# A spectral convolution and two gated MLPs on one core: output tiles through the two input buffers, sums of weight blocks in smaller pieces

## The chip, the cores and the metric

The kernel runs on one core of one Trainium2 chip. The metric is the device time of one execution in microseconds (us), the median of several runs. Engines are named as in the profile: PE is TensorE's matmul, PEld its weight load, DVE VectorE, ACT ScalarE, POOL GpSimd, SP SyncE, which here issues nearly all DMAs.

## The reference

```python
X = np.fft.rfft(x, axis=1)                    # x: 2 x 3008 x 256
y = np.fft.irfft(X * (filt_r + 1j * filt_i), n=3008, axis=1)
x = y.reshape(6016, 256)
gate = 1.0 / (1.0 + np.exp(-(x @ w_gate)))    # w_gate, w_val: 256 x 1536
x = gate * (x @ w_val) @ w_out                # first MLP
h = x @ w_in                                  # w_in: 256 x 2048
g = h * (1.0 / (1.0 + np.exp(-1.702 * h)))
out = g @ w_out2                              # second MLP
```

## The kernel before

Tokens lie along the free dimension in 12 tiles of 512 or 480 columns. The convolution of the first batch comes first, the first MLP over its tiles and beside it the convolution of the second batch follow, and from about 710 us on the second MLP runs alone. Each product of 128 rows is made of three matmuls (`mm3`, lines 120 to 122): every float32 operand is held as a high part, made by ACT (line 116), and a remainder, the low part, made by POOL or DVE (line 117).

The second MLP takes the tiles in six pairs `p`, and for each pair the 2048 rows of `w_in` in eight sets `fp` of two blocks. The two by two blocks of a set are multiplied with seven products in place of eight: `prod(o, k, first)` adds product `k` to one of the four banks `x`, `z`, `y`, `w`. Their left sides are blocks of `w_in` and sums of such blocks (`w_parts`, `combine_w`); their right sides are input tiles and sums of input tiles (`x_parts`, `combine_x`). A set then has four results, each a `Block`: `sig` is ACT's sigmoid of the bank into `sg`, `mul` is DVE's product of bank and `sg` (line 742), `parts` the split into high (ACT) and low (POOL), and `back(c)` the product of the result with a block of `w_out2`, added to the accumulator `accs[j][c]`. The eight `back` products of a set run between the seven `prod` of the next, so the last ones of a pair run in set 0 of the next pair.

PE, ACT, DVE and POOL keep the order of the program in this stage (it is under `manual_schedule`), and SP does so everywhere. Before this stage a planner orders the other engines.

When the last `back(0)` of a tile is done, ACT copies the accumulator into the output tile `outs[t]`, for `back(1)` DVE does, and SP sends each half out (lines 753 to 759). That tile has the tag `o` with `bufs=1`: one buffer, which the tile's two halves share, and which the next tile's copies get once its DMAs are done. The inputs of a pair are read by `load_x2` into tiles of the tag `yraw`, which has two buffers (`new_raw`, line 405): SP is asked for the next pair's in set 1, and `combine_x` reads them from set 3 on.

The sums that `combine_w` and `combine_x` make are spread over the sets as `chores`, a list of steps. `chore()` takes the next step; it stands at three places of a set: place 1 after the previous set's last `parts`, place 2 after `bz.parts`, place 3 after `bw.parts`. `combine_w` for the weights of sets 0 to 4 is called in the last tile of the first MLP, all steps at once; for sets 5 to 7 its steps are appended in sets 0, 1 and 2 of pair 0. The twelve steps of `combine_x` for the next pair are appended in set 3 of pairs 0 to 4. The tiles that `combine_w` and `combine_x` use for their intermediate sums have the same tags, `ex` and `c`, with one buffer each.

Of the kernel before, what the change touches and what calls it, by code (L numbers as in the profile page):

```python
# [8 lines left out]
F32 = mybir.dt.float32  # L9
# [3 lines left out]
AF = mybir.ActivationFunctionType  # L13
# [4 lines left out]
P = 128  # L18
# [69 lines left out]
def kernel(  # L88
# [12 lines left out]
    nc = tc.nc  # L101
# [3 lines left out]
    work = ctx.enter_context(tc.tile_pool(name="work", bufs=2))  # L105
# [13 lines left out]
    def mm3(o, w, x, first, last, **kw):  # L119
        nc.tensor.matmul(out=o, lhsT=w[0], rhs=x[0], start=first, stop=False, **kw)  # L120
        nc.tensor.matmul(out=o, lhsT=w[0], rhs=x[1], start=False, stop=False, **kw)  # L121
        nc.tensor.matmul(out=o, lhsT=w[1], rhs=x[0], start=False, stop=last, **kw)  # L122
# [248 lines left out]
    nt = len(tiles)  # L371
    pos = [0]
# [31 lines left out]
    def new_raw():  # L404
        return work.tile([P, 2, 512], F32, tag="yraw", name="yraw")
# [17 lines left out]
    def load_x2(t):  # L423
        raw = new_raw()
        nc.sync.dma_start(out=raw, in_=xscr[t].rearrange("(c p) n -> p c n", p=P))
        return raw
# [37 lines left out]
    def w_parts(fp):  # L464
        f0, f1 = slice(2 * fp * P, (2 * fp + 1) * P), slice((2 * fp + 1) * P, (2 * fp + 2) * P)

        def spare(k):
            a, b = divmod(3 * fp + k, 8)
            c, d = divmod(b, 4)
            return [e[:, c, d * P:(d + 1) * P] for e in extra[a]]  # L470

        a11, a12, a22, s1 = ([w[:, c, f] for w in wi] for c, f in ((0, f0), (1, f0), (1, f1), (0, f1)))
        return a11, a12, spare(2), a22, s1, spare(0), spare(1)

    def combine_w(fp):
        fs = slice(2 * fp * P, (2 * fp + 2) * P)
        v = stage[0].tile([P, 2, 2, P], F32, tag="ex", name="wv")
        r = stage[0].tile([P, 4, P], F32, tag="c", name="wr")
        q = w_parts(fp)
        dst = q[4], q[5], q[6], q[2]  # L480

        def sums():
            nc.vector.tensor_add(v.rearrange("p c i f -> p c (i f)"), *[w[:, :, fs].bitcast(F32) for w in wi])
            nc.vector.tensor_add(r[:, 0], v[:, 0, 1], v[:, 1, 1])
            nc.vector.tensor_sub(r[:, 1], r[:, 0], v[:, 0, 0])
            nc.vector.tensor_sub(r[:, 2], v[:, 0, 0], v[:, 0, 1])
            nc.vector.tensor_sub(r[:, 3], v[:, 1, 0], r[:, 1])

        def hi():
            for k in range(4):  # L490
                nc.scalar.activation(out=dst[k][0], in_=r[:, k], func=AF.Copy)

        def lo():
            for k in range(4):
                nc.vector.tensor_sub(dst[k][1], r[:, k], dst[k][0].bitcast(F32))  # L495

        return [sums, hi, lo]

    def x_parts(p):
        if p % 2 == 0:  # L500
            at = [[w[:, k].rearrange("p v c f -> p (v c f)") for w in wg] for k in range(7)]
        else:
            at = [[w[:, 7 + k].rearrange("p v c f -> p (v c f)") for w in wg] for k in range(5)]
            at += [[w[:, 2 * k:2 * k + 2, :].rearrange("p a b -> p (a b)") for w in wo] for k in range(2)]
        return at

    def combine_x(p, raw):
        n = tiles[2 * p][3]
        (b11, b21), (b12, b22) = ([r[:, c, :n] for c in range(2)] for r in raw)
        dst = [[w[:, :n] for w in d] for d in x_parts(p)]  # L510
        u, v = (stage[0].tile([P, 512], F32, tag=k, name="xs")[:, :n] for k in ("ex", "c"))

        def hi(k, src):
            nc.scalar.activation(out=dst[k][0], in_=src, func=AF.Copy)

        def lo(k, src):
            nc.vector.tensor_sub(dst[k][1], src, dst[k][0].bitcast(F32))

        sub = nc.vector.tensor_sub
        return [  # L520
            lambda: hi(0, b11),
            lambda: (lo(0, b11), hi(1, b21)),
            lambda: (lo(1, b21), hi(2, b22)),
            lambda: lo(2, b22),
            lambda: sub(u, b12, b11),
            lambda: (sub(v, b22, u), hi(4, u)),
            lambda: (lo(4, u), hi(5, v)),
            lambda: lo(5, v),
            lambda: sub(b12, b22, b12),
            lambda: (sub(u, b21, v), hi(6, b12)),  # L530
            lambda: (lo(6, b12), hi(3, u)),
            lambda: lo(3, u),
        ]
# [113 lines left out]
    for t in range(2, nt):  # L647
        for f in range(FC1):
            steps = []
            if pools is not None:  # L650
                k, odd = divmod(unit, 2)
# [54 lines left out]
            if f in (0, 2, 4, 6, 8):  # L706
                for step in combine_w(f // 2):
                    step()
            if f == 6:
                raw = [load_x2(u) for u in range(2)]  # L710
            if f == 8:
                sums = combine_x(0, raw)
# [16 lines left out]
    outs = {}  # L729

    class Block:
# [15 lines left out]
        def back(self, c):  # L747
            t, n, f = self.t, self.n, 2 * self.fp + self.i
            last = self.fp == FC2 // 2 - 1 and self.i == 1
            cs = slice(c * P, (c + 1) * P)  # L750
            acc = accs[self.j][c][:, :n]
            mm3(acc, [w[:, f, cs] for w in wp], self.gp, self.fp == 0 and self.i == 0, last)
            if last:
                if c == 0:
                    outs[t] = work.tile([P, 2, 512], F32, tag="o", name="o", bufs=1)
                    nc.scalar.copy(outs[t][:, 0, :n], acc)  # L756
                else:
                    nc.vector.tensor_copy(outs[t][:, 1, :n], acc)
                nc.sync.dma_start(out=out[c * P:(c + 1) * P, pos[t]:pos[t] + n], in_=outs[t][:, c, :n])

    backs = [pend[0], None, pend[1]]
    chores = []
# [8 lines left out]
    def chore():  # L771
        if chores:
            chores.pop(0)()

    for p in range(nt // 2):
        n = tiles[2 * p][3]
        for fp in range(FC2 // 2):
            z, y, w, x = (ps[(nset + k) % 4][:, :n] for k in (1, 2, 3, 0))
            g = gring[nset % 2 * 4:nset % 2 * 4 + 4]
            bz, by, bw, bx = (  # L780
                Block(i, j, p, fp, o, q) for (i, j), o, q in zip(((0, 0), (0, 1), (1, 1), (1, 0)), (z, y, w, x), g)
            )
            nset += 1
            lhs, rhs = w_parts(fp), x_parts(p)

            def prod(o, k, first):
                mm3(o, lhs[k], [r[:, :n] for r in rhs[k]], first, True, skip_group_check=True)

            if p == 0 and fp < 3:
                chores += combine_w(5 + fp)  # L790
            if p + 1 < nt // 2:
                if fp == 1:
                    raw = [load_x2(2 * p + 2 + u) for u in range(2)]
                if fp == 3:
                    chores += combine_x(p + 1, raw)

            prod(x, 0, True)
            if prev:
                prev.mul()
            nc.scalar.copy(s1[:, :n], x)  # L800
            back()
            if prev:
                prev.parts()
            chore()
            prod(z, 1, True)
            back()
            nc.vector.tensor_add(z, z, s1[:, :n])
            bz.sig()
            prod(y, 4, True)
            bz.mul()  # L810
            prod(x, 5, False)
            nc.scalar.copy(s5[:, :n], y)
            nc.scalar.copy(s2[:, :n], x)
            back()
            bz.parts()
            chore()
            prod(y, 2, False)
            nc.vector.tensor_add(y, y, s2[:, :n])  # L818
            by.sig()
            back()  # L820
            prod(x, 6, False)
            nc.vector.tensor_add(w, x, s5[:, :n])  # L822
            bw.sig()
            back()
            by.mul()
            by.parts()
            back()
            bw.mul()
            bw.parts()
            back()  # L830
            chore()
            prod(x, 3, False)
            bx.sig()
            back()
            prev = bx
            backs = [lambda o=o, c=c: o.back(c) for o in (bz, by, bw, bx) for c in range(2)]
    prev.mul()
# [43 lines left out]
```

## Time and profile before

| | |
|---|---|
| median of 3 runs | 1220.15 us (1218.12 to 1223.8) |
| the profiled execution | 1219.74 us |
| its span, first to last instruction | 1217.8 us |
| PE busy | 1169.5 us, 96% |
| DVE, ACT, POOL busy | 681.5 us (56%), 659.0 us (54%), 573.4 us (47%) |
| mean granted clock of TensorE | 0.99 |

The profile is of one execution. Busy times are unions over the engine's instructions; matmuls are pipelined, and their modelled ends reach into the next one's start. A wait is the idle time of an engine before an instruction, put down to what ended it.

### The profile page before, as it was taken

The page shows a single profiled execution, that of the slowest core. Times are in us where ns is not written, and L with a number is a line of the kernel's source. Part 1 is how long each engine was busy: PE and PEld are TensorE (multiplying, and loading weights), DVE is VectorE, ACT ScalarE, POOL GpSimd, SP SyncE. Part 2 cuts the span into 40 slices and gives each one's busy share as a digit, 9 for nine tenths or more (in the row PEclk, how much of TensorE's full clock was granted, in tenths as well). Part 3 has the DMA queues.
Part 4 walks back from the last instruction along what each step waited for, and adds up shares of the span by engine and source line. Part 5 has one row for each costly group of instructions (what it writes and reads, how often), then busy time and mean ns, then how long its engine had stood idle before and what let it go on. Part 6 is the DMA issues. An engine that isn't in the chain of part 4 may idle for free.

```text
span 1217.8 us, 14310 instructions
## 1 busy us (share of the span) xinstructions
PE 1169.5 (96%) x5072; PEld 951.0 (78%) x5072; DVE 681.5 (56%) x1055; ACT 659.0 (54%) x1171; POOL 573.4 (47%) x456
## 2 busy tenths in 40 slices
PE   8869899999999999999999989999999999999998
PEld 3447688887878888888888867878888888788886
DVE  7889944565553552452744547645546556555443
ACT  5445544565653443343433446666666666666664
POOL 6622314666653542433433334545545555455453
PEclk9979999999999999999999999999999999999999
DMA  7444501222202121120210110020010010200000
GB/s 183 117 153 131 129 1 60 53 74 68 71 14 79 51 87 52 35 87 15 72 35 1 52 52 1 1 70 1 1 70 1 25 44 1 70 1 1 35 1 33
DMA packets 31351, 61.73 MB, mean 51 GB/s; under 512 B 3088, under 2 KB 10512, under 8 KB 31280
## 3 DMA queue, kind: packets, MB, share of 16 engines
q1 hardware_dynamic: 30992, 60.57, 16.6%
q8 instruction: 39, 0.64, 0.2%
q10 hardware_dynamic: 288, 0.26, 0.1%
q14 instruction: 32, 0.26, 0.1%
HBM read 42.20 MB, written 17.69 MB: 49 GB/s over the span
## 4 chain that ended last, share of the span: by engine, by line
PE 85%; DVE 8%; issue 3%; DMA 2%; ACT 1%; POOL 1%; SPq 0%; ACTq 0%; DVEq 0%; POOLq 0%
PE ps L120 28%; PE ps L122 28%; PE ps L121 28%; DMA out_dram<-o 1%; DVE m L161 1%; DVE c L164 1%; PE ps L257 1%; DVE m L158 1%; DVE m L168 1%; DVE g L117 1%; DVE ps L392 0%; DVE yp L495 0%; DMA f<-in_fd_dram 0%; DVE y L282 0%; DVE z L292 0%
## 5 line engine op out<-in xcount | busy, mean ns | idle before, releaser
L117 POOL TENSOR_TENSOR g<-sg,g 128x512 fp32r<-128x512 f32 (+1 forms) x216 | 282.2, 1311 | 396.1 <-ACT g L116 383.2
L120 PE MATMUL ps<-yp,wg 128*128 128x512 f32 (+1 forms) x576 | 225.4, 391 | 14.5 <-ACT yp L116 7.8
L121 PE MATMUL ps<-yp,wg 128*128 128x512 f32 (+1 forms) x576 | 224.2, 389 | 4.3 <-POOL yp L117 4.3
L122 PE MATMUL ps<-yp,wg 128*128 128x512 f32 (+1 forms) x576 | 223.6, 388 | 0.0
L116 ACT ACTIVATE g<-sg 128x512 fp32r<-128x512 f32 (+1 forms) x216 | 134.6, 623 | 123.2 <-DVE sg L395 111.1
L742 DVE TENSOR_TENSOR sg<-ps,sg 128x512 f32<-128x512 f32 (+1 forms) x192 | 130.0, 677 | 114.9 <-ACT sg L739 109.0
L739 ACT ACTIVATE sg<-ps 128x512 f32<-128x512 f32 (+1 forms) x192 | 113.2, 590 | 140.9 <-DVE ps L818 42.8
L117 POOL TENSOR_TENSOR wo<-sg,wo 128x512 fp32r<-128x512 f32 (+1 forms) x96 | 126.3, 1326 | 116.4 <-ACT wo L116 102.6
L395 DVE TENSOR_TENSOR sg<-ps,sg 128x512 f32<-128x512 f32 (+1 forms) x120 | 80.8, 674 | 158.0 <-PE ps L122 151.1
L120 PEld LDWEIGHTS ps<-yp,wg 128*128 128x128 f32 x576 | 109.0, 189 | 39.1 <-DVE g L117 9.9
L389 ACT ACTIVATE sg<-ps 128x512 f32<-128x512 f32 (+1 forms) x144 | 84.1, 584 | 89.6 <-POOL g L117 47.2
L121 PEld LDWEIGHTS ps<-yp,wg 128*128 128x128 f32 x576 | 109.0, 189 | 25.3 <-POOL yp L117 5.2
L122 PEld LDWEIGHTS ps<-yp,wg 128*128 128x128 f32 x576 | 108.9, 189 | 21.0
L122 PE MATMUL ps<-g,wo 128*128 128x512 f32 (+1 forms) x288 | 111.7, 388 | 0.0
L121 PE MATMUL ps<-g,wo 128*128 128x512 f32 (+1 forms) x288 | 111.6, 388 | 0.0
L120 PE MATMUL ps<-g,wo 128*128 128x512 f32 (+1 forms) x288 | 111.6, 388 | 0.0
L120 PE MATMUL ps<-g,wp 128*128 128x512 f32 (+1 forms) x192 | 74.8, 390 | 6.4 <-ACT o L756 6.4
L120 PE MATMUL ps<-wg,wi 128*128 128x512 f32 (+1 forms) x192 | 74.1, 386 | 0.8 <-DVE ps L822 0.8
L122 PE MATMUL ps<-g,wp 128*128 128x512 f32 (+1 forms) x192 | 74.3, 387 | 0.0
L121 PE MATMUL ps<-g,wp 128*128 128x512 f32 (+1 forms) x192 | 74.2, 387 | 0.0
L121 PE MATMUL ps<-wo,wp 128*128 128x512 f32 (+1 forms) x192 | 74.1, 386 | 0.0
L122 PE MATMUL ps<-wo,wp 128*128 128x512 f32 (+1 forms) x192 | 74.1, 386 | 0.0
(152 smaller groups left out, 2192.1 us busy)
## 6 DMA issues: line engine op xcount, KB each, us to landing
raw<-in_w_out_dram SPq DMA_DIRECT2D x14, 512.0 KB, 3.8
f<-in_fd_dram SPq DMA_DIRECT2D x16, 384.0 KB, 4.7
xscr<-x SPq DMA_DIRECT2D x12, 512.0 KB, 3.2
yraw<-xscr SPq DMA_DIRECT2D x12, 512.0 KB, 4.9
x<-in_xd_dram SPq DMA_DIRECT2D x15, 384.0 KB, 4.6
yscr<-tt SPq DMA_DIRECT2D x40, 128.0 KB, 2.2
yraw<-yscr SPq DMA_DIRECT2D x10, 512.0 KB, 5.4
raw<-in_w_in_dram SPq DMA_DIRECT2D x8, 512.0 KB, 3.6
```

The lines of the kernel that those rows point to most:

```text
L116: nc.scalar.activation(out=dst_hi, in_=src, func=AF.Copy)
L117: lo_eng.tensor_sub(dst_lo, src, dst_hi.bitcast(F32))
L120: nc.tensor.matmul(out=o, lhsT=w[0], rhs=x[0], start=first, stop=False, **kw)
L121: nc.tensor.matmul(out=o, lhsT=w[0], rhs=x[1], start=False, stop=False, **kw)
L122: nc.tensor.matmul(out=o, lhsT=w[1], rhs=x[0], start=False, stop=last, **kw)
L158: nc.vector.tensor_scalar(m, hw, 0xFFFFF, 0x100000, op0=ALU.bitwise_and, op1=ALU.bitwise_or)
L161: nc.vector.scalar_tensor_tensor(out=f, in0=lw, scalar=2.0**-32, in1=m, op0=ALU.mult, op1=ALU.add)
L164: nc.vector.scalar_tensor_tensor(out=cu, in0=hw, scalar=0x80000000, in1=cu, op0=ALU.bitwise_and, op1=ALU.bitwise_or)
L389: nc.scalar.activation(out=sg[:, :n], in_=sig_src[:, :n], func=AF.Sigmoid, scale=scale)
L395: nc.vector.tensor_mul(sg[:, :n], val_src[:, :n], sg[:, :n])
L739: nc.scalar.activation(out=self.sg, in_=self.bank, func=AF.Sigmoid, scale=1.702)
L742: nc.vector.tensor_mul(self.sg, self.bank, self.sg)
```

## The change

It does two things. The output tiles of the second MLP are taken from the tag `yraw`, which has two buffers, in place of `o`, which has one; for the last two tiles the first half's DMA is issued by ACT in place of SP. And the steps of `combine_w` become five in place of three, each with fewer instructions, with a fourth place for `chore()` at the end of a set, after the last `back()`; the fourth place takes steps of `combine_x` too. Both use the same instructions on the same engines as before.

```diff
-        def sums():
+        def whole():
             nc.vector.tensor_add(v.rearrange("p c i f -> p c (i f)"), *[w[:, :, fs].bitcast(F32) for w in wi])
-            nc.vector.tensor_add(r[:, 0], v[:, 0, 1], v[:, 1, 1])
-            nc.vector.tensor_sub(r[:, 1], r[:, 0], v[:, 0, 0])
-            nc.vector.tensor_sub(r[:, 2], v[:, 0, 0], v[:, 0, 1])
-            nc.vector.tensor_sub(r[:, 3], v[:, 1, 0], r[:, 1])
-
-        def hi():
-            for k in range(4):
-                nc.scalar.activation(out=dst[k][0], in_=r[:, k], func=AF.Copy)
-
-        def lo():
-            for k in range(4):
-                nc.vector.tensor_sub(dst[k][1], r[:, k], dst[k][0].bitcast(F32))
-
-        return [sums, hi, lo]
+
+        def sums(k):
+            if k == 0:
+                nc.vector.tensor_add(r[:, 0], v[:, 0, 1], v[:, 1, 1])
+                nc.vector.tensor_sub(r[:, 1], r[:, 0], v[:, 0, 0])
+            else:
+                nc.vector.tensor_sub(r[:, 2], v[:, 0, 0], v[:, 0, 1])
+                nc.vector.tensor_sub(r[:, 3], v[:, 1, 0], r[:, 1])
+
+        def hi(k):
+            nc.scalar.activation(out=dst[k][0], in_=r[:, k], func=AF.Copy)
+
+        def lo(k):
+            nc.vector.tensor_sub(dst[k][1], r[:, k], dst[k][0].bitcast(F32))
+
+        return [
+            whole,
+            lambda: sums(0),
+            lambda: (hi(0), hi(1), sums(1)),
+            lambda: (lo(0), lo(1), hi(2), hi(3)),
+            lambda: (lo(2), lo(3)),
+        ]
...
             if last:
                 if c == 0:
-                    outs[t] = work.tile([P, 2, 512], F32, tag="o", name="o", bufs=1)
-                    nc.scalar.copy(outs[t][:, 0, :n], acc)
+                    outs[t] = new_raw()
+                o = outs[t][:, c, :n]
+                if c == 0:
+                    nc.scalar.copy(o, acc)
                 else:
-                    nc.vector.tensor_copy(outs[t][:, 1, :n], acc)
-                nc.sync.dma_start(out=out[c * P:(c + 1) * P, pos[t]:pos[t] + n], in_=outs[t][:, c, :n])
+                    nc.vector.tensor_copy(o, acc)
+                (nc.scalar if t >= nt - 2 and c == 0 else nc.sync).dma_start(
+                    out=out[c * P:(c + 1) * P, pos[t]:pos[t] + n], in_=o
+                )
...
             prod(x, 3, False)
             bx.sig()
             back()
+            chore()
             prev = bx
```

## Rows read from the trace of the kernel before

**Rows 1.** The page's first part: busy time of each engine, share of the span

```profile
PE 1169.5 (96%) x5072; PEld 951.0 (78%) x5072; DVE 681.5 (56%) x1055; ACT 659.0 (54%) x1171; POOL 573.4 (47%) x456
```

**Rows 2.** PE's waits, 480 us to end: who, for whom, total us, times, longest

```profile
PE ps L120 <- ACT o L756: 6.4, 5, 1.3
PE ps L120 <- ACT s L812: 5.7, 2, 3.6
PE ps L120 <- DVE ps L822: 0.8, 1, 0.8
```

**Rows 3.** Timeline at a boundary of pairs: start, us, instruction [idle before <-releaser]

```profile
807.20 0.63 ACT L116 ACTIVATE g<-sg 128x512 fp32r<-128x512 f32 x1 [0.29 <-DVE sg L742]
...
808.17 0.39 PE L122 MATMUL ps<-wg,wi 128*128 128x512 f32 x1
809.22 0.58 ACT L756 COPY o<-ps 128x512 f32<-128x512 f32 x1 [1.40 <-DMA out_dram<-o]
...
809.86 0.50 PE L120 MATMUL ps<-g,wp 128*128 128x512 f32 x1 [1.31 <-ACT o L756]
```

**Rows 4.** PE in set 1; by windows: busy PE, PEld, DVE, ACT, POOL, clock, DMA

```profile
726.97 0.79 PE L120 MATMUL ps<-wg,yp 128*128 128x512 f32 x1 [3.64 <-ACT s L812]
...
726.97:729.70 2.73, 2.73 (x7) 2.15 (x8) 0.89 (x2) 1.94 (x7) 1.29 (x1) 0.50 0.00 0
...
740.83:743.50 2.67, 2.67 (x12) 2.21 (x13) 1.18 (x3) 2.35 (x7) 1.30 (x1) 1.00 0.00 0
```

**Rows 5.** Timeline of DVE and ACT before that wait in set 1

```profile
718.85 0.28 DVE L495 TENSOR_TENSOR wi<-wr,wi 128x128 fp32r<-128x128 f32 x1
719.05 2.89 DVE L495 TENSOR_TENSOR yp<-wr,yp 128x128 fp32r<-128x128 f32 x3
...
722.46 0.68 DVE L483 TENSOR_TENSOR wv<-wi,wi 128x512 f32<-128x512 f32 x1
...
725.06 0.69 DVE L807 TENSOR_TENSOR ps<-ps,s 128x512 f32<-128x512 f32 x1
...
726.34 0.58 ACT L812 COPY s<-ps 128x512 f32<-128x512 f32 x1
```

**Rows 6.** Timeline of DVE and POOL at the end of set 2

```profile
745.44 1.38 DVE L495 TENSOR_TENSOR yp<-wr,yp 128x128 fp32r<-128x128 f32 x1
...
746.63 1.34 POOL L117 TENSOR_TENSOR g<-sg,g 128x512 fp32r<-128x512 f32 x1
```

**Rows 7.** Timeline of POOL, DVE, ACT, PE from set 3's end into set 4

```profile
755.54 0.68 DVE L517 TENSOR_TENSOR wg<-yraw,wg 128x512 fp32r<-128x512 f32 x1
755.54 1.84 POOL L117 TENSOR_TENSOR wo<-sg,wo 128x512 fp32r<-128x512 f32 x1 [2.08 <-ACT wo L116]
...
757.34 1.30 POOL L117 TENSOR_TENSOR wo<-sg,wo 128x512 fp32r<-128x512 f32 x1
...
758.05 0.69 DVE L742 TENSOR_TENSOR sg<-ps,sg 128x512 f32<-128x512 f32 x1 [1.82 <-ACT sg L739]
...
760.53 0.58 ACT L812 COPY s<-ps 128x512 f32<-128x512 f32 x1
...
761.47 0.39 PE L120 MATMUL ps<-wg,yp 128*128 128x512 f32 x1
761.70 0.39 PE L121 MATMUL ps<-wg,yp 128*128 128x512 f32 x1
```

**Rows 8.** Timeline of the end, landing of the out DMAs, ACT's second DMA issue

```profile
1211.83 0.38 PE L122 MATMUL ps<-wo,wp 128*128 128x480 f32 x1
...
1213.73 0.66 DVE L758 COPY o<-ps 128x480 f32<-128x480 f32 x1 [2.13 <-DMA out_dram<-o]
1214.30 0.81 SPq L759 DMA_DIRECT2D out_dram<-o  x2
...
DMA to landing us min/median/max: 2.0/2.1/3.6
...
1.18 0.45 ACTq L547 DMA_DIRECT2D tabs<-in_tab_dram  x1
```

## The prediction, made before the changed kernel was run

> **What bounds the kernel now.** I began with the page's first part: PE is busy 96% of the span [rows 1], so what PE does not do sets the end, and a change off PE pays only where PE waits. The change touches the last 508 us (the sets of the second MLP) and a few sums before them. So I asked next for PE's waits from 480 us to the end. There are three kinds and no other [rows 2]: 6.4 us in 5 waits for the copies of line 756, 5.7 us in 2 waits for the copy of line 812, and one of 0.8 us. Then I opened each in the timeline. From one matmul's start to the next is 0.23 us while a row shows 0.39 (761.47 to 761.70, [rows 7]): ends are modelled and overlap, so a wait costs its shown idle plus 0.16 us.
>
> The boundary of two pairs [rows 3], shown at 809 us, occurs five times. ACT's second copy into `o` begins at 809.22 after 1.40 us of waiting for the DMA that empties the one buffer; PE's next product needs the bank which that copy reads and starts at 809.86. The idle time is 6.4/5 = 1.28, with the 0.16 it is 1.44, and the first matmul after it takes 0.50 in place of 0.39: 1.55 us a boundary, 7.75 us for five.
>
> The sums of weights in sets 1 and 2 of the first pair [rows 4, 5]. In set 1 PE idles 3.64 us before the second product into `y`, until ACT's copy `s5` (726.34) is out. That copy stands behind `bz.sig`, this behind DVE's `z` add (725.06), and DVE comes to that add late: after `bw.mul` it does four small `lo` subtractions (718.85 to 721.94), then `prev.mul`, then the five `sums` (722.46 to 725.06). Behind the wait TensorE's granted clock is 0.50, the lower level of 1.2 GHz, for 2.73 us. It had idled 3.64 us before that; after the other wait (5.7 - 3.64, 2.06 us idle in set 2) the stretch from 740.83 has the upper level. So set 1 loses 3.64 + 0.16 of wait and half of 2.73, 1.37, at the clock: 5.2 us; set 2 loses 2.06 + 0.16 + 0.1 = 2.3 us. The 0.8 us wait of set 0 follows DVE's `w` add right after PE's own product; nothing of the change stands in front of it, and it stays.
>
> **Boundary buffers: what goes.** The second `o` copy takes the other `yraw` buffer and waits for no DMA. What is late next is ACT itself: the copy stands behind `bw.parts`, whose ACT half runs 807.20 to 807.83 [rows 3]. So it runs about 807.80 to 808.38 and releases PE some 0.06 us later, as 809.80 to 809.86 shows now. PE wants the bank at 808.17 + 0.23 = 808.40. I leave 0.1 us a boundary: 7.75 - 0.5 = 7.2 us gained. DVE's copy of the other half has no wait either, and its `prev.mul` comes sooner.
>
> What the two buffers cost: SP's two `load_x2` of the next set now wait for the out DMAs of the same buffers. Those land 2.1 us after issue [rows 8]. Nothing but these loads is queued on SP, and the combination that reads them starts two sets later (a set is 45 matmuls of 0.23, some 10 us), so I cost it at nothing; without that cover it would cost the 2.1 us of one landing, once a pair. The buffers' former readers, the combination steps, end in set 5 or 6, before set 0 of the next pair.
>
> **End of the kernel.** The last matmul starts at 1211.83, and DVE's last copy waits until 1213.73 for the shared buffer; its DMA issue stands as second on SP, whose two issues from 1214.30 take 0.81 us, so it begins near 1214.7 [rows 8]. Without the wait the copy starts as the last matmul ends, near 1212.25, ends at 1212.9, and SP, whose queue holds only the `c == 1` halves, issues at 1212.95: 1.8 us. The last stretch's issues by ACT are bounded by ACT's issue at the start of the kernel, 0.45 us [rows 8]: with a copy of at most 0.66 it fits into the six matmuls, 1.3 us, between ACT's two last copies. Bounds: 1.3 us (one such issue in the way) to 2.2.
>
> **Smaller pieces.** Counted on DVE between `bw.mul` and the `z` add. Set 1 now: 4 `lo`, `prev.mul`, 5 `sums`. After: places 3 and 4 of set 0 give 4 small pieces (two subtractions, two `lo`), then `prev.mul`, then 2 small `lo`. The first part keeps its length, for POOL's two splits run there; in the second 0.5 us stands for 2.6, so the `z` add moves 2.1 us earlier, and `s5` with it. The wait falls from 3.8 to about 1.7 us and the clock, as after 2.06 us idle, should hold: 5.2 - 1.8 = 3.4 gained. ACT's `hi` pieces of place 4 stand behind `bx.sig` and push the copy `s1` by 0.5 us, which that `z` add doesn't yet need. Set 2: 4 small pieces before `prev.mul`, 0.5 us after it in place of 2.6; `s5` comes 2.1 earlier less about 0.1 for two `hi` now before `bz.sig`: 2.2 gained. Set 3 receives pieces of the last block where the old order had none before the `z` add (two subtractions, two `hi`, 1.0 us) against some 0.7 us of room: 0.3 lost. Sum 5.3 us, bounds 1 (pieces blocked as below) to 7.
>
> In later pairs the steps of `combine_x` move from three places in four sets to four places in three. Nothing is added, but a DVE step now stands directly before `prev.mul`. Today's place 3 [rows 7]: DVE's step and POOL's `by` split start together at 755.54, POOL's takes 1.84 in place of 1.30, its next runs to 758.64; DVE then idles until `prev.mul` at 758.05. A step at place 4 becomes ready near 756.85 (ACT's `hi` before it), is held to POOL's end at 757.38, takes its 0.6 and is out at about 757.95: before `prev.mul`. That DVE gets in between two POOL operations is in [rows 6]: a small subtraction held from 745.44 on ended at 746.82, just as POOL's second split, begun at 746.63, took the port. I cost these 12 sets at nothing; if the step loses to the second split too, it holds `prev.mul` from 758.05 to about 759.25, and `s5` (out at 761.11, wanted at 761.47) comes about 0.8 late where a place-1 step follows, 0.2 where none does.
>
> The five sums before the last stage are placed by the planner; of PE's waits after 480 us [rows 2] none lies before 716 us, and they change order only. Nothing, with 1 us either way kept in the range.
>
> A rule of the Trainium skill speaks against the change: SBUF — State Buffer, "Who interferes with whom", says that a VectorE operation with two SBUF inputs and a GpSimd operation that reads SBUF hold one port exclusively, and whichever is second fully blocks. The rows agree (1.38 against 0.28 us for the same subtraction, [rows 5, 6]). By it alone every place-4 step would block behind POOL's pair of splits; that result is the third and fourth rival below.
>
> **Sum.** 7.2 + 1.8 + 5.3 = 14.3 us off the profiled execution's own 1219.74 (span 1217.8 and 1.9 around it): 1205.4. The median of the three runs, 1220.15, is within 0.03% of that execution, so no shift.
>
> **Rivals.**
> 1. The boundary wait stays in another form, as the planner hands out buffers by what is free and the second copy still waits for a DMA. For: nothing in the trace shows which buffer is given. Against: both were last read some 20 us earlier. Gain 1.8 + 5.3: 1212.6. Chance 0.07.
> 2. Pieces in sets 0 to 3 are each blocked behind a POOL split, and the wait only moves to other sets. For: the 1.38 us of [rows 6]. Against: the 0.28 us of [rows 5], and two pieces behind `prev.mul` meet no split there. Gain 9.0 + 1: 1209.7. Chance 0.08.
> 3. The place-4 steps of `combine_x` lose to both splits: in pairs 1 to 4 0.8 + 0.8 + 0.2 each, in pair 0 0.8 + 0.8, in all 8.8 us given back: 1214.2. Against: [rows 6]. Chance 0.08.
> 4. Slower than before: DVE loses the port at place 3 as well, whenever POOL has a split queued. Then both steps run after 758.2, `prev.mul` ends near 760.1 and `s5` near 762.9, 1.5 us late. 17 sets have a DVE piece at place 4 (5 in pair 0, 12 later): 25.5 lost against 14.3, 1231. It decides from 14.3/17 = 0.84 us a set. Against: at 755.54 DVE wins the port. Chance 0.04.
>
> **How the numbers follow.** The forecast has 0.73. A measurement of this kernel tells 0.5%, 6.1 us, from no change. Faster by more: forecast, rivals 1 and 2, 0.88; within: rival 3, 0.08; slower: 0.04. The range reaches down to full gains at the boundaries, the end and set 1 (17 us), and up past rivals 1 and 2: 1202 to 1213.
>
> **What would show it.** Right: ACT's and DVE's copies of `o` wait for no DMA; PE's waits for line 756 under 0.5 us in all; one wait for line 812 of 1.5 to 2 us in set 1, no granted clock of 0.50 near 727; the span ends some 4.2 us after the last matmul's start where it was 6.0. Wrong: PE waits for line 812 in sets 4 to 6 of each pair, with `prev.mul` behind a DVE row of more than 1.2 us; or new waits of PE before 710 us.

## The result, and the profile after

The changed kernel takes 1211.18 us (median of 5 runs, 1207.47 to 1212.18) against 1223.14 us for the kernel before, measured again beside it (5 runs, 1218.12 to 1223.8): ratio 0.9911, 95% interval 0.9886 to 0.9935. That is 12 us less, where 14.3 were forecast. The direction was right, the time lies inside the range, and one term of the sum, that of the smaller pieces, was too large.

The profiled execution of the changed kernel took 1212.18 us, its span is 1210.1 us. This group is PE's waits from 480 us on (who, for whom, total us, times, longest), and answers [rows 2]:

```profile
PE ps L120 <- DVE ps L834: 2.2, 1, 2.2
```

The waits for the copy of the output (five) and for the copy `s5` (two) are gone. The one of set 0, for DVE's `w` add, has grown from 0.8 to 2.2 us.

The boundary of pairs 0 and 1 in the timeline, which answers [rows 3] (ACT's second copy of an output, DVE's, PE's next product into that bank):

```profile
808.27 0.63 ACT L116 ACTIVATE g<-sg 128x512 fp32r<-128x512 f32 x1 [0.29 <-DVE sg L750]
...
808.80 0.57 ACT L766 COPY yraw<-ps 128x512 f32<-128x512 f32 x1
808.98 0.69 DVE L768 COPY yraw<-ps 128x512 f32<-128x512 f32 x1 [0.75 <-PE ps L122]
...
809.24 0.39 PE L122 MATMUL ps<-wg,wi 128*128 128x512 f32 x1
...
809.46 0.46 PE L120 MATMUL ps<-g,wp 128*128 128x512 f32 x1
```

ACT's copy starts at 808.80, as its own high part ends (the rows overlap by 0.1 us, to 808.90), and waits for no DMA; DVE's waits for PE's product alone. PE goes from 809.24 to 809.46 in its normal step of 0.22.

The end, which answers the timeline in [rows 8]:

```profile
1206.05 0.38 PE L122 MATMUL ps<-wo,wp 128*128 128x480 f32 x1
...
1206.41 0.35 ACTq L769 DMA_DIRECT2D out_dram<-yraw  x1
1206.47 0.66 DVE L768 COPY yraw<-ps 128x480 f32<-128x480 f32 x1 [0.65 <-PE ps L122]
...
1207.16 0.33 SPq L769 DMA_DIRECT2D out_dram<-yraw  x1
```

The last copy follows the last matmul after 0.42 us, where it came 1.9 us after it, and its DMA is issued at once.

**A measure that leaves the first 710 us out.** The second MLP's first matmul starts at 709.94 us before and at 714.91 after; 3.5 us of that difference are there when the first MLP starts (56.77 and 60.25), long before anything that the change touches. The other 1.5 us arise before 385 us: from the 1300th matmul of the first MLP (379.7 us before, 384.6 after) to the start of the second, all ten profiles of this case take 330.28 us, to 0.01 us. So the new order of the weight sums among the work of the first MLP costs PE nothing. Over the ten profiles that start lies between 709.9 and 714.9, in two of the changed kernel at 713.5 and 714.9. So below I also give the stage time: the span's end less that start. It is 1217.8 - 709.9 = 507.9 us before and 495.2 after: 12.7 us gained, and a second profile of the changed kernel gives 495.1.

### The profile page after: what moved, and what is told of

The parts are those of the page before. It is cut to its first block, busy times and chain, and to the rows that moved or that the text cites. A ratio compares the mean times of both kernels' runs of the same rounds, so it can differ in the third digit from the quotient of the medians.

```text
span 1210.1 us, 14295 instructions
## 1 busy us (share of the span) xinstructions
PE 1170.2 (97%) x5072; PEld 949.5 (78%) x5072; DVE 694.9 (57%) x1055; ACT 659.3 (54%) x1171; POOL 575.7 (48%) x456
## 4 chain that ended last, share of the span: by engine, by line
PE 88%; DVE 8%; DMA 2%; issue 1%; POOL 0%; ACT 0%; SPq 0%; DVEq 0%; POOLq 0%; ACTq 0%
PE ps L120 29%; PE ps L121 29%; PE ps L122 29%; DVE m L161 2%; DMA f<-in_fd_dram 1%; DVE c L164 1%; DVE m L168 1%; PE ps L299 1%; DVE ps L392 1%; DVE m L158 1%; DVE g L117 0%; DVE ex L153 0%; DVE z L292 0%; PE ps L289 0%; DVE a L259 0%
## 5 line engine op out<-in xcount | busy, mean ns | idle before, releaser
L117 POOL TENSOR_TENSOR wo<-sg,wo 128x512 fp32r<-128x512 f32 (+1 forms) x96 | 130.0, 1364 | 111.1 <-ACT wo L116 90.5
L120 PE MATMUL ps<-wg,wi 128*128 128x512 f32 (+1 forms) x192 | 74.4, 388 | 2.2 <-DVE ps L834 2.2
L121 PE MATMUL ps<-wg,wi 128*128 128x512 f32 (+1 forms) x192 | 74.6, 388 | 0.0
L122 PE MATMUL ps<-wg,wi 128*128 128x512 f32 (+1 forms) x192 | 74.4, 388 | 0.0
```

The source lines that it names most:

```text
L117: lo_eng.tensor_sub(dst_lo, src, dst_hi.bitcast(F32))
```

## The experiments

Lost time means what the starts of successive matmuls in the last stage are apart beyond the normal 0.23 us (0.22 for 480 columns), summed from the timeline. Each ratio is to the kernel before, measured beside that kernel on the same chip: 1223.14 us for the changed kernel, 1221.95 for e1 to e4, 1221.82 for e5, e6 and the two repeats. Differences of stage times are taken before rounding.

| kernel | median us (runs) | ratio to before, 95% interval | stage time us | lost us |
|---|---|---|---|---|
| before | see above | | 507.9 | 16.4 |
| changed | 1211.18 (5) | 0.9911, 0.9886 to 0.9935 | 495.2 | 5.3 |
| e1_buffers | 1212.56 (4) | 0.9921, 0.9908 to 0.9934 | 499.0 | 9.4 |
| e2_pieces | 1218.92 (10) | 0.9976, 0.9964 to 0.9987 | 504.5 | 12.9 |
| e3_first_sums | 1207.24 (5) | 0.9888, 0.9873 to 0.9903 | 493.5 | 3.8 |
| e4_early_hi | 1207.60 (4) | 0.9881, 0.9866 to 0.9895 | 493.0 | 3.2 |
| e5_place1 | 1222.16 (10) | 1.0002, 0.9989 to 1.0014 | 508.4 | 18.4 |
| e6_sp_only | 1208.87 (1) | | 495.2 | 5.3 |
| changed_again | 1209.68 (6) | 0.9898, 0.9883 to 0.9914 | 495.1 | 5.3 |
| e4_again | 1207.39 (5) | 0.9882, 0.9867 to 0.9896 | 493.1 | 3.2 |

**Each half alone.** The first kernel takes the output part of the change and leaves the sums as they were.

```diff
-                    outs[t] = work.tile([P, 2, 512], F32, tag="o", name="o", bufs=1)
+                    outs[t] = new_raw()
...
-                nc.sync.dma_start(
+                (nc.scalar if t >= nt - 2 and c == 0 else nc.sync).dma_start(
```

> The kernel before with the output buffers alone (two yraw buffers, ACT issuing for the last two tiles); sums and chores as before. Stage time means: from the first matmul of the second MLP to the end of the span; it was 507.9 us before and 495.2 with the whole change. Theory A, that the buffers carry the five boundaries (7.6) and the end (1.9) and nothing else: 498.4 us, no wait of PE for the copies of o, while the two waits for the copy of line 812 (5.7 us idle) and the granted clock of 0.50 in set 1 stay. Ratio to before about 0.992. Rival B, that the boundary waits were already half hidden and come back elsewhere once the pieces are not spread: 501 to 504 us, with new waits of PE in sets 0 and 1 of pairs 1 to 5.

Measured: stage time 499.0. PE's waits:

```profile
PE ps L120 <- ACT s L816: 5.0, 2, 3.6
PE ps L120 <- DVE ps L826: 0.8, 1, 0.8
```

(Columns as above.) No wait for the copies of an output is left, and nothing new in later pairs, so rival B falls: the output buffers, by the boundaries and the end, carry 8.9 us of stage time. It is 0.6 us less than theory A said, for one reason that shows: after the 3.6 us wait of set 1 the granted clock stays at its lower level for twice as long as before,

```profile
726.50:733.30 6.80, 5.44 (x13) 4.29 (x14) 2.72 (x5) 3.88 (x10) 1.28 (x1) 0.50 0.00 0
```

(a window of that stretch: its length, busy PE, PEld, DVE, ACT, POOL, then the clock, 0.50). Six more matmuls at 0.43 in place of 0.23 cost some 1.3 us, and set 2's wait shrinks by 0.7.

The second kernel takes the smaller pieces and the fourth place, and keeps the one buffer.

```diff
-                    outs[t] = new_raw()
+                    outs[t] = work.tile([P, 2, 512], F32, tag="o", name="o", bufs=1)
```

> The smaller pieces and the fourth place alone; outputs through the one buffer o as before. Theory A: the five boundary waits stay (6.4 us idle for the copy of o), sets 0 to 3 lose 4.4 us in place of 8.5 as with the whole change, so stage time about 504 us against 507.9, ratio 0.996 to 0.998. Rival B, that the pieces gain the 5.3 us that were forecast and something in the later pairs takes 2 us back: waits in sets 3 to 6 of pairs 1 to 4 that add up to 2 us. Rival C, that the pieces alone bring nothing: 507 to 508.

Measured: stage time 504.5, 3.4 us gained. PE's waits:

```profile
PE ps L120 <- ACT o L764: 6.4, 5, 1.3
PE ps L120 <- DVE ps L830: 2.2, 1, 2.2
```

The boundary waits are all there, the two for `s5` are gone, and set 0 waits 2.2 us, as in the whole change. In the sets that carry steps of `combine_x` the lost time is 0.1 us in each of 6 (two of pair 0, four of pairs 2 and 3), not 2 us in all, so rival B falls, and C with it. The two halves add up: 8.9 + 3.4 = 12.3 of the 12.7 us. So the term that was forecast too large is that of the pieces (5.3), and the shortfall lies in the first sets.

**Set 0.** The timeline of the changed kernel, DVE and POOL before PE's wait of set 0, and PE:

```profile
720.43 0.66 DVE L443 COPY x<-ps 128x480 f32<-128x480 f32 x1 [0.49 <-PE ps L122]
721.00 0.28 DVE L487 TENSOR_TENSOR wr<-wv 128x128 f32<-128x128 f32 x1
721.32 1.35 DVE L488 TENSOR_TENSOR wr<-wr,wv 128x128 f32<-128x128 f32 x1
722.59 0.69 DVE L830 TENSOR_TENSOR ps<-ps,s 128x512 f32<-128x512 f32 x1
723.19 0.68 DVE L834 TENSOR_TENSOR ps<-ps,s 128x512 f32<-128x512 f32 x1
...
721.25 1.27 POOL L117 TENSOR_TENSOR g<-sg,g 128x512 fp32r<-128x512 f32 x1 [4.77 <-ACT g L116]
...
723.93 0.50 PE L120 MATMUL ps<-wg,wi 128*128 128x512 f32 x1 [2.18 <-DVE ps L834]
```

The second of the two small sums is held by POOL's split, takes 1.35 us in place of 0.28, and the `y` and `w` adds come after it. In the kernel before these sums were not here: its timeline of DVE shows all five of this block among the work of the first MLP,

```profile
686.60 0.69 DVE L483 TENSOR_TENSOR wv<-wi,wi 128x512 f32<-128x512 f32 x1
...
688.49 0.29 DVE L484 TENSOR_TENSOR wr<-wv 128x128 f32<-128x128 f32 x1
688.82 1.20 DVE L485 TENSOR_TENSOR wr<-wr,wv 128x128 f32<-128x128 f32 x1
689.94 0.28 DVE L486 TENSOR_TENSOR wr<-wv 128x128 f32<-128x128 f32 x1
690.14 0.28 DVE L487 TENSOR_TENSOR wr<-wv,wr 128x128 f32<-128x128 f32 x1
```

some 20 us before the stage starts. They are DVE's first instructions in the fixed order and need nothing of the stage, so the order that is kept in the stage did not hold them back. With the smaller pieces only the first step is found there in the changed kernel,

```profile
691.86 0.69 DVE L483 TENSOR_TENSOR wv<-wi,wi 128x512 f32<-128x512 f32 x1
```

and the second stands behind `x2`'s copy (line 443) and `bz.mul`, which need PE. The third kernel gives the first step of that one block all its sums again.

```diff
+        if fp == 5:
+            return [
+                lambda: (whole(), sums(0), sums(1)),
+                lambda: None,
+                lambda: (hi(0), hi(1)),
+                lambda: (lo(0), lo(1), hi(2), hi(3)),
+                lambda: (lo(2), lo(3)),
+            ]
```

> The whole change, but for the block of set 5 alone all sums are in the first step (so that nothing of them stands behind set 0's own work), the second step is empty; the rest of the steps at the places of the change. Theory A, that the 2.2 us wait of set 0 and the granted clock of 0.50 after it come from the two small sums at place 2 of set 0: that wait falls to 0.8 us idle, the clock stays at its upper level, and a wait of about 1.2 us idle for the copy s5 comes back in set 1, which the late set 0 had covered; stage time 493.9 against 495.2. Rival, that set 0 waits because of its missing back products and the two sums only fill that time: 2.2 us idle and the clock of 0.50 stay, 495.2.

Measured: stage time 493.5, 1.6 us less than the changed kernel. PE's waits:

```profile
PE ps L120 <- ACT s L832: 1.1, 1, 1.1
PE ps L120 <- DVE ps L842: 0.8, 1, 0.8
```

The window of its sets 0 and 1 (length, busy PE, PEld, DVE, ACT, POOL, clock, DMA):

```profile
710.41:730.00 19.59, 17.73 (x76) 13.83 (x75) 12.57 (x21) 12.55 (x26) 8.13 (x7) 1.00 0.23 81
```

The five sums run before the stage again (687.02 to 690.84). Set 0 waits 0.8 us again, the wait for `s5` is back with 1.1 us, and the clock, 1.00 in the window, does not fall. So the two small sums made set 0's wait, and the rival falls.

The fourth kernel moves that block's other pieces too.

```diff
+                lambda: (whole(), sums(0), sums(1)),
+                lambda: (hi(0), hi(1), hi(2), hi(3)),
+                lambda: (lo(0), lo(1)),
+                lambda: None,
+                lambda: (lo(2), lo(3)),
```

> As the run before this one, and the block's four high parts at place 2 of set 0, two low parts at place 3, nothing at place 4, two low parts at place 1 of set 1. Theory A: set 0 waits 0.8 us idle; in set 1 two small subtractions fewer stand before prev.mul, so the z add comes some 0.5 us sooner than in the run before and the wait for s5 falls to 0.5 to 0.8 us; stage time 492.8 us, the shortest of all, ratio to before 0.987 to 0.990. Rival: set 1's wait is set by POOL's splits, which hold the next sigmoid, and not by DVE's pieces: then it stays at 1.2 us and stage time at 493.9.

Measured: stage time 493.0; the wait for `s5` is 0.7 us. The timeline of DVE from `bw.mul` to the `z` add:

```profile
723.16 0.28 DVE L497 TENSOR_TENSOR wi<-wr,wi 128x128 fp32r<-128x128 f32 x1
723.36 0.29 DVE L497 TENSOR_TENSOR yp<-wr,yp 128x128 fp32r<-128x128 f32 x1
725.46 0.69 DVE L758 TENSOR_TENSOR sg<-ps,sg 128x512 f32<-128x512 f32 x1 [1.81 <-ACT sg L755]
726.07 0.48 DVE L497 TENSOR_TENSOR yp<-wr,yp 128x128 fp32r<-128x128 f32 x2
726.47 0.69 DVE L827 TENSOR_TENSOR ps<-ps,s 128x512 f32<-128x512 f32 x1
```

The two pieces of place 3 slip in ahead of POOL, and `prev.mul` now waits 1.81 us for ACT's sigmoid: DVE is no longer what makes that product late. The sigmoid starts at 724.83, after 0.91 us of waiting for POOL's first split, which ends at 724.80. Both theories named a part: 0.5 us came off, and what is left follows the chain of POOL's split and that sigmoid; that the two low parts between `prev.mul` and the `z` add (0.4 us) hold a part of it too was not tried.

**The fourth place.** The next kernel has the same steps, four a set, but the fourth right behind the first.

```diff
             chore()
+            chore()
             prod(z, 1, True)
...
             back()
-            chore()
             prev = bx
```

> The whole change, but the fourth chore of a set is taken at place 1, right behind the first, in place of the end of the set: same pieces, same number a set, none between bw.mul and prev.mul beyond place 3. Theory A, that the end of a set is free room (DVE idles there until prev.mul) and place 1 is not, where s5 has 0.36 us to spare: two steps at place 1 delay the z add by 0.7 us and bz.sig by 0.6 more, so PE waits about 1.0 us for the copy s5 in each of sets 3 to 5 of pairs 0 to 4, 15 waits; stage time 495.2 + 8 to 16 us. Rival, that DVE has room anywhere in a set and only the number of steps counts: no such waits, 495 us.

Measured: stage time 508.4, all of the gain lost (ratio 1.0002). PE's waits:

```profile
PE ps L120 <- ACT s L825: 11.7, 13, 1.5
PE ps L120 <- DVE ps L835: 1.0, 1, 1.0
```

In pairs 1 to 4 the three sets with steps lose about 1.2, 0.5 and 0.4 us each, in pair 0 seven sets 1.2 to 1.8. So the place counts and not the number of steps. The estimate of 1.0 in each of 15 sets was right in sum (13.3 us of stage time, within the 8 to 16) and not in its spread. In this kernel set 0's first two small sums run before the stage (689.37 and 689.70), so set 0 loses 1.3 us and not the 4.0 of the changed kernel. In the changed kernel's timeline the steps at the end of a set look like this (set 4 of pair 1; POOL's two splits, DVE's step, `prev.mul`):

```profile
848.54 1.80 POOL L117 TENSOR_TENSOR g<-sg,g 128x512 fp32r<-128x512 f32 x1 [2.08 <-ACT g L116]
...
850.30 1.71 POOL L117 TENSOR_TENSOR g<-sg,g 128x512 fp32r<-128x512 f32 x1
...
849.81 1.04 DVE L525 TENSOR_TENSOR wg<-xs,wg 128x480 fp32r<-128x480 f32 x1 [0.63 <-ACT wg L522]
851.00 0.69 DVE L750 TENSOR_TENSOR sg<-ps,sg 128x512 f32<-128x512 f32 x1 [0.15 <-ACT sg L747]
```

DVE's step is held until POOL's first split ends at 850.34, ends at 850.85, POOL's second split takes 1.71 in place of 1.30, and `prev.mul` still waits for ACT and not for DVE. The trace shows the same order in all twelve sets of pairs 1 to 4 that carry such steps: DVE's step takes 1.03 to 1.09 us, POOL's second split 1.66 to 1.74.

**The end.** SP issues every output DMA:

```diff
-                (nc.scalar if t >= nt - 2 and c == 0 else nc.sync).dma_start(
+                nc.sync.dma_start(
```

> The whole change, but SP issues all output DMAs, the last two tiles' first halves too. Theory A, that the end gained its 1.9 us from the copies that wait for no DMA: SP's issue of the first half is over before the last copy ends, and from the last matmul's start to the end of the span stay 4.0 us. Rival, that ACT's issue beside SP's carries part of it: 4.4 us.

Measured: 4.03 us from the last matmul's start to the span's end, as with ACT's issue (4.02; 6.00 before). So in this one run the issue by ACT brings nothing; the missing wait brings the 2.0 us.

**The two best side by side.**

> The changed kernel itself, beside the run with the early high parts on the same chip. Its stage time was 495.2 us. Expected of theory A: 495 us again, 1.5 to 2.5 us more than with the early high parts; the first 710 us, which the change does not touch, spread by several us from run to run in both.

> The early high parts again, beside the changed kernel. Theory A: stage time 493.0, 2.1 us less than the changed kernel, ratio to it about 0.998; rival, that the difference belongs to the chip of the earlier runs: stage times equal.

Measured: 1209.68 us (6 runs) and 1207.39 us (5 runs), stage times 495.1 and 493.1, so the early high parts beat the changed kernel by 2.0 us of stage time and about 0.2% in the medians. The intervals against the kernel before overlap, so the medians alone don't separate the two; the stage time repeats within 0.2 us in the two profiles of each kernel, and the reading rests on that. The rival, that the difference belongs to the chip of the earlier runs, falls. The start of the second MLP was at 713.48 and 712.10, within the spread named above.

## Why the prediction was right, and where it was off

The table compares the terms of the sum, in us of stage time; lost time is worked out from the matmuls' starts.

| step | forecast | measured |
|---|---|---|
| five boundaries | 7.2 | 7.6: 7.75 lost before, 0.14 after |
| the end | 1.8 | 2.0: 6.00 to 4.02 |
| sets 0 to 3 of pair 0 | 5.3 | 4.1: 8.7 lost before, 4.5 after |
| `combine_x` at place 4 | 0 | -0.6: 0.1 in each of 6 sets |
| sum | 14.3 | 13.1; by stage time 12.7, the rest in gaps under 0.05 us |

**The boundaries and the end** went as worked out: ACT's copy runs behind its own high part, PE keeps its normal step, the last DMA is issued when the last copy ends. Of the 0.1 us a boundary that I kept back, 0.03 was lost. The SP loads behind the out DMAs cost nothing that shows; no engine waits for them.

**The step that failed** is the sentence that the 0.8 us wait of set 0 stays, since "nothing of the change stands in front of it". I had read the sums of set 0's block as lying in set 0, where [rows 5] shows only its `lo` subtractions, and did not look for where its five sums ran. They ran some 20 us before the stage. Once they are split into steps, the second step stays in set 0, behind `x2`'s copy and ahead of the `y` add. That made the wait 1.4 us longer, and then the clock fell, where I had reasoned from set 2 that some 2 us idle leave it alone:

```profile
721.37:723.93 2.56, 0.38 (x3) 0.00 (x1) 2.50 (x3) 0.56 (x1) 1.15 (x1) 1.00 0.74 234
724.90:728.30 3.40, 3.40 (x9) 2.65 (x9) 2.90 (x6) 2.89 (x8) 2.69 (x2) 0.50 0.54 198
```

(windows of the changed kernel: the wait, and the 3.40 us at a clock of 0.50 behind it, the lower level of 1.2 GHz; the matmuls start 0.43 us apart there in place of 0.23, which costs about 1.5 us.) This wait and the clock thus took 4.0 us where I had left 1.1. Against that, set 1's wait of 1.7 us did not come, as PE arrived there 3.0 us later than in my walk. That the one miss made good more than half of the other is luck. Two of the signs I had named did not show: the wait of 1.5 to 2 us in set 1, and no clock of 0.50 near 727. With the sums back in their old place (e3_first_sums) set 1 idles 1.06 us and loses 1.24 + 0.11: the walk for set 1 had the right wait, somewhat too long. Sets 2 and 3 lost 0.1 and 0.3 us, as forecast.

**Place 4.** That DVE's step gets in between POOL's two splits, the point on which rivals 3 and 4 hung, holds in the rows above, and the price of 0.8 us a set was not paid. Where steps do stand at a bad place there is a price: e5_place1 lost about as much as the whole change had gained.

The Trainium skill's rule from SBUF — State Buffer, "Who interferes with whom", that the second of the two operations blocks until the first is done, agrees with each of these rows (1.35 for 0.28 us in set 0, 1.71 for 1.30 at place 4). Which goes first when DVE's step and POOL's second split both stand in line, the rows show: here DVE's step did, and a further piece behind it then waited for that split.

**Of the rivals** none came true as a whole. By the gain of 12.0 us alone, forecast (14.3) and rival 2 (10.0) fit about equally; the waits tell them apart. The second output did get the other buffer (rival 1). Of rival 2 a part holds: pieces of 0.28 us were blocked behind POOL's splits in all of sets 0 to 3; this is DVE at the ends of sets 0, 1 and 2:

```profile
726.90 1.37 DVE L497 TENSOR_TENSOR yp<-wr,yp 128x128 fp32r<-128x128 f32 x1
...
737.01 1.38 DVE L490 TENSOR_TENSOR wr<-wv 128x128 f32<-128x128 f32 x1
...
746.56 1.27 DVE L487 TENSOR_TENSOR wr<-wv 128x128 f32<-128x128 f32 x1
```

But PE lost 0.1 and 0.3 us in sets 2 and 3, and the blocked piece that made a wait is the one in front of set 0's adds.

The medians' 12.0 us lie below the stage time's 12.7 by less than the spread of the first 710 us.

## What to carry to other kernels

Before an operation list is split into steps, look up where the whole list runs now: here the planner could start the fixed order early, which hid its first step only, and what became the second step stayed behind the work ahead of it. Small pieces were cheap where the engine waits anyway, here at the end of a set (at most 0.1 us in a set with `combine_x`), and cost 0.3 to 1.8 us a set where the next consumer has 0.4 us to spare (e5_place1). And one output buffer between two engines that drain at different moments is worth a look at every boundary: here PE waited 1.3 us at each of five boundaries for a copy that stood behind a DMA's landing, and a buffer that lay idle at that time took these waits out.

## What was not expected of the hardware

TensorE's granted clock fell to 0.50 after a wait of 2.18 us idle in set 0, in all four profiles of kernels with that wait, and not after 2.03 us idle in set 2 of the kernel before, nor after 1.06 us in e3_first_sums; it stayed down 3.4 us, and 6.8 us in e1_buffers after a wait of 3.6 us like the one that brought 3.4 us of it in the kernel before. What decides between these was not tried. For a wait of some 2 us both outcomes are thus on record here: nothing at the clock, and about 1.5 us.
